# Turned tiles split on VectorE, score groups every eight products, and a first block whose first four places carry no scores

## The chip, the cores and the metric

The kernel runs on one core of one Trainium2 chip. The metric is the device time of one execution in microseconds (us). Before the change it is 1717.77 us, the median of three runs (1717.59 to 1717.90).

## What is computed

```python
def reference(A_x, A_wqkv, A_wo, B_x, B_w_gate, B_w_up, B_w_down):
    xn = _layernorm(A_x)                       # 2048 tokens of 512
    qkv = (xn @ wqkv)                          # 32 heads of 16
    p = softmax(q @ k.T * 16 ** -0.5)          # per head, 2048 x 2048
    s = (p @ v) @ wo
    g = silu(((xn @ w_gate) * (xn @ w_up)) @ w_down)   # 1792 wide
    return A_x + s * g
```

## The kernel before, in words

Every fp32 factor is split into a high and a low part, so that a product is the sum of three: high by high, high by low, low by high. Tokens are 16 tiles of 128, in four chunks (c = 0 to 3) of four tiles. Heads are taken in groups of four; a round is one head group and one chunk of queries.

**The early part** (`early`, L705) makes the layer norm, the keys and queries of the first head pair and all values. It is one stream of 253 steps n: the products of keys and queries of chunk 0, values of tiles 0 to 2, keys of chunk 1 (n = 60 to 71), queries of chunk 1 (72 to 83), values of tile 3, keys of chunk 2 (96 to 107), values of tiles 4 and 5, keys of chunk 3 (132 to 143), and values of tiles 6 to 14. One product is one matmul of 128 x 512. A table `at` says ahead of which n other work is put into the engines' queues: statistics (`ln_stats`, VectorE), normalisation (`ln_apply`, on VectorE for odd tiles under 8, else on ScalarE), and the turn of a tile (`ln_turn`): four transpositions on TensorE into one PSUM bank of tag "x", of which there are two, then on ScalarE a copy `raw` (L249) and the high part `xh` (L250), and on GpSimd the low part `xl` as raw less high (line L63, through which all of GpSimd's and SyncE's calls go). Chunk 0 goes another way: ScalarE writes the high part and VectorE subtracts it from the PSUM bank itself (`ln_low`, L258).

The list `EARLY` (L40) names the steps ahead of which a group of four **own scores** is computed: four matmuls of 48 rows (L609) into four PSUM banks of tag "s", each followed by a maximum on VectorE (`mx`, L611). These scores serve only to find the row maxima. Groups 0 to 3 read the keys of chunk 0, groups 4 to 7 those of chunk 1, groups 8 to 11 those of chunk 2, groups 12 to 15 those of chunk 3. After 64 scores `maxima(0)` reduces them on VectorE and sends the result through DRAM (MD) into the rows of the queries (`qs`).

Keys of a chunk go a long way before a score can read them: ScalarE takes the high part `hl` (L306) and a copy `qr` (L309) out of PSUM, GpSimd subtracts, SyncE stores both parts in DRAM (KD) and, when these have landed, loads them back in another layout (`ks`).

**The main part** runs through 2048 places q (`position`, L904). A place computes the scores of one key tile for one head again, turned (L631), and their exponentials on ScalarE (L633), and beside it one own score of a place that lies LEAD = 86 further on. Turned scores and values share three PSUM banks of tag "st"; own scores now have three. A filler puts the products of projections and of the feed-forward part (L285 and L289, two halves of 64 rows) between the places. Every eight places or so a block multiplies the exponentials with the values (L644). Four places stand ahead of the first block without filler.

All five engines take their instructions in the order in which the program writes them.

Of the kernel before, what the change touches and what calls it, by code (L numbers as in the profile page):

```python
# [22 lines left out]
NC = S // 512  # L23
# [8 lines left out]
LEAD = 86  # L32
CYCLES = 240
AHEAD = range(1, 5)
# [2 lines left out]
EBUFS = 11  # L37
HBUFS = 2
QBUFS = 2
EARLY = [66, 75, 84, 93] + [104 + 37 * n // 4 for n in range(17)]  # L40
EARLY_BUFS = {"s": 4, "x": 2, "f": 2}
BUFS = {"st": 3, "s": 3, "misc": 2}
LOWER, UPPER = slice(0, 64), slice(64, P)
# [5 lines left out]
def body(ctx, tc, x, wqkv, wo, wg, wu, wd, out):  # L49
# [23 lines left out]
    def dma(dst, src):  # L73
        sync.dma_start(dst, src)
# [41 lines left out]
    def psum(tag, name):  # L116
        ps, bufs = fst["ps"]
        return ps.tile([P, 512], F32, tag=tag, name=name, bufs=bufs[tag])
# [45 lines left out]
    def wtile(name):  # L164
        return keep.tile([P, ND, P], F32 if name[-1] == "r" else F32R, name=name, bufs=1 if name[-1] == "r" else 2)
# [19 lines left out]
    def tokens(tt):  # L185

        return raw_x[:, tt] if tt < 8 else V[:, tt, 0:D]

    def load_x(tt):
        dma(tokens(tt), x[tt * P:(tt + 1) * P])  # L190
# [38 lines left out]
    def ln_apply(tt):  # L229
        (mv, r0, e, mr), t = norm[tt]  # L230
        xt = tokens(tt)
        if tt < 8 and tt % 2:
            return nc.vector.tensor_scalar(xt, xt, e[:, t:t + 1], mr[:, t:t + 1], op0=OP.mult, op1=OP.add)
        return nc.scalar.activation(xt, xt, AF.Identity, bias=mr[:, t:t + 1], scale=e[:, t:t + 1])

# [4 lines left out]
    def ln_turn(tt):  # L240
        c, t = divmod(tt, 4)
        xt = tokens(tt)
        norm["x", tt] = pt = psum("x" if c else "s", f"xT{tt}")
        for d in range(ND):
            nc.tensor.transpose(pt[:, d * P:(d + 1) * P], xt[:, d * P:(d + 1) * P], ident)
        hi, lo = [x[c][:, :, t * P:(t + 1) * P] for x in (xh, xl)]
        if c:
            raw = norm["raws"][t]
            nc.scalar.activation(raw, pt, AF.Copy)  # L249
            nc.scalar.activation(hi, pt.rearrange("p (d q) -> p d q", d=ND), AF.Copy)  # L250
            pool.tensor_tensor(lo, raw.rearrange("p (d q) -> p d q", d=ND), hi, op=OP.subtract)
        else:
            nc.scalar.activation(hi, pt.rearrange("p (d q) -> p d q", d=ND), AF.Copy)
# [452 lines left out]
    def early():  # L706

        nc.scalar.activation(look, ones[0:1, 0:1], AF.Sqrt)
        for tt in range(4):
            load_x(tt)  # L710
        wraw = []
        for which in (1, 0):
            wraw.append(wtile(f"w{which}r"))
            dma(wraw[-1], wqkv[:, which * D:which * D + P].rearrange("(d p) f -> p d f", p=P))
        norm["raws"] = raws = [etile() if d < 3 else part_tile() for d in range(ND)]
        for d in range(ND):
            dma(raws[d], wqkv[d * P:(d + 1) * P, 2 * D:])
        for tt in range(4, NT):
            load_x(tt)

        def ahead(m):
            fst["qk", m] = qk_weights(m, 1), qk_weights(m, 0)

        def exp_table(_):
            nc.scalar.activation(look, ones[0:1, 0:1], AF.Exp)

        def warm(n):
            for _ in range(n):
                nc.tensor.matmul(psum("x", "warm"), ident, idle, start=True, stop=True)

        warm(4)
        first = (0, 1), (2, 3)
        for tts in first:
            ln_open(tts)
        ln_stats(0)
        ln_stats(1)
        ln_root(first[0])
        ln_scale(first[0])
        ln_apply(0)
        ln_apply(1)  # L740
        ln_stats(2)
        ln_stats(3)
        ln_turn(0)
        ln_turn(1)
        warm(3)
        ln_root(first[1])
        ln_scale(first[1])
        ln_apply(2)
        last = ln_apply(3)
        ln_low(0)  # L750
        ln_low(1)
        ln_turn(3)
        ln_turn(2)
        ln_low(3)
        ln_low(2)
        wk, wq = [split_raw(f"w{which}", raw, last) for which, raw in zip((1, 0), wraw)]
        wv = [[etile().bitcast(F32R) for _ in range(ND)] for _ in range(2)]
        for d in range(ND):
            nc.scalar.activation(wv[0][d], raws[d], AF.Copy)
            pool.tensor_tensor(wv[1][d], raws[d], wv[0][d], op=OP.subtract)  # L760

        def k(c):
            yield from qk_proj(wk, 0, 1, c, "f")
            load_k(0, [c])

        def q(c):
            yield from qk_proj(wq, 0, 0, c, "f" if c else "x")
            load_q(c)

        def v(*tts):  # L770
            for tt in tts:
                yield from v_proj(wv, tt, "f")

        at = {n: [] for n in range(253)}
        for c, stats, apply, turns in ((1, (0, 2, 4, 6), (26, 26, 26, 26), (38, 42, 46, 50)),
                                       (2, (16, 20, 26, 27), (60, 60, 62, 62), (70, 74, 79, 83)),
                                       (3, (30, 34, 36, 38), (73, 73, 85, 85), (100, 106, 112, 118))):
            for t in range(4):
                for n, fn in ((stats[t], ln_stats), (apply[t], ln_apply), (turns[t], ln_turn)):
                    at[n].append((fn, 4 * c + t))  # L780
        for tts, n, root, scale in ((tuple(range(4, 8)), 0, 13, 25), (tuple(range(8, NT)), 16, 52, 53)):
            at[n].insert(0, (ln_open, tts))
            at[root].append((ln_root, tts))
            at[scale].insert(0, (ln_scale, tts))
        at[190].append((ones_rows, ks[0]))
        at[150].append((exp_table, None))
        at[205].append((ahead, 1))
        at[130] += [(ones_columns, slice(8, NT)), (other_keys, None)]
        fst["v"] = v_proj(wv, NT - 1, "st")
        gens = [k(0), q(0), v(0, 1, 2), k(1), q(1), v(3), k(2), v(4, 5), k(3), v(*range(6, NT - 1))]  # L790
        scored = 0
        stream = (n for g in gens for n in g)
        for n in range(253):
            for fn, arg in at[n]:
                fn(arg)
            if n in EARLY:
                for _ in range(4 if n != EARLY[-1] else LEAD - scored):
                    score(scored, 0)
                    scored += 1
                if scored == 64:  # L800
                    maxima(0)
            next(stream, None)
        assert scored == LEAD
        return wq

    ffp = ExitStack()
# [105 lines left out]
    def position(q):  # L912

        n, j = divmod(q, 4)
        i, kt = divmod(n, NT)
        g, c = divmod(i, NC)
        now[0] = n
        Tied.on = n < 18
        if j == 0:
            if kt == 8 and i + 2 < NU:  # L920
                load_q(i + 2)
            if kt == 0 and g + 1 < NG and c == 1:
                load_k(g + 1)
            ready[n] = i, kt, []
        if j == 3 and kt % 4 == 2:
            step_small(later)
        ready[n][2].append(expo(i, kt, j))
        scored = q + LEAD
        if scored < TOTAL:
            score(scored, 1)  # L930
        step()
        if j == 1:
            prepare()
        if scored < TOTAL and scored % (4 * NT) == 4 * NT - 1:
            reduced.append(lambda: maxima(scored // (4 * NT)))

    TOTAL = NU * NT * 4

    with tc.manual_schedule(engines=ORDERED):
# [2 lines left out]
        ctx.enter_context(banks_of(BUFS))  # L942
        run(fst["v"])
        q = 0
        while q < 4:
            position(q)
            q += 1
        for b in range(NU * NT // 2):
            if fil.done:
                parts = iter([3, 2, 3, 2, 2, 2, 1, 2])  # L950
                fil = Filler(ending(), lambda n: next(parts))
            work = fil.begin()
            if b >= NU * NT // 2 - 2:
                last = TOTAL - 4 * (NU * NT // 2 - 1 - b)
            else:
                fits = min(9, max(7, int(2.6 + 0.62 * work))) if q + LEAD < TOTAL and work else 8
                need = 8 * (b + 1)
                last = min(max(q + fits, need + AHEAD[0]), need + AHEAD[-1], TOTAL - 4)
            count = last - q
            fil.spread(max(2, count - 2))  # L960
            for k in range(count):
                position(q)
                q += 1
                if 0 < k < count - 1 or count < 3:
                    fil.part()
            if b < NU * NT // 2 - 1:
                values([ready.pop(2 * b), ready.pop(2 * b + 1)])
# [33 lines left out]
```

## Time and profile before

| | before |
|---|---|
| median of three runs | 1717.77 us |
| the profiled execution | 1718.17 us |
| its span, first to last instruction | 1716.4 us |
| granted TensorE clock | 0.999 |
| early part, first matmul to first turned score | 2.4 to 101.0 us |
| first block of value products starts | 108.2 us |

In a row of the timeline stand the start in us, the duration in us, the engine, the line, the operation, output and inputs, and how many instructions were merged into the row. Brackets give idle time of that engine ahead of it and what ended it. PE is TensorE, DVE VectorE, ACT ScalarE, POOL GpSimd, SPq the queue of SyncE that issues transfers. A row's duration of several matmuls counts the last one to its end; the next row can start before.

### The profile page before, as it was taken

To read this page: it belongs to the slowest core of one execution; us is meant where nothing else is said; L and a number is where in the kernel's file an instruction comes from. 1 tells how busy PE (TensorE), PEld (TensorE's weight loads), DVE (VectorE), ACT (ScalarE), POOL (GpSimd) and SP (SyncE) were. 2 spreads that over 40 slices of the span, in tenths; PEclk is the share of its full clock that TensorE was granted. 3 is DMA by queue.
4 is the path that set the end of the run, shared out by engine and by line. 5 is a ranking of instruction groups with operands and counts; after the bars stand their busy time and mean duration, and the time that the engine had idled before them with its cause. 6 is when DMAs were issued, how large, how long until landed. Compare 5 with 4: busy or idle time off the path is not lost. (4 is left out here: it accounts for less than half of the span.)

```text
span 1716.4 us, 35005 instructions
## 1 busy us (share of the span) xinstructions
PE 1705.0 (99%) x13574; PEld 1042.5 (61%) x13574; DVE 1435.9 (84%) x2478; ACT 1307.4 (76%) x2568; POOL 885.4 (52%) x889
## 2 busy tenths in 40 slices
PE   8999999999999999999999999999999999999998
PEld 6666656666666665666656565666665666666655
DVE  6778888888888888888888888888888888898933
ACT  6358877877777778778777777887778787777774
POOL 5315445762644638446354572663637546446572
PEclk9999999999999999999999999999999999999999
DMA  6316633620241312412115220320225112011352
GB/s 210 106 48 201 243 115 125 152 66 19 64 91 36 107 47 73 89 47 60 30 52 133 64 74 23 92 71 27 64 75 125 54 36 73 27 54 48 121 177 79
DMA packets 117378, 145.79 MB, mean 85 GB/s; under 512 B 12636, under 2 KB 74332, under 8 KB 114524
## 3 DMA queue, kind: packets, MB, share of 16 engines
q1 hardware_dynamic: 117212, 143.55, 28.5%
q8 instruction: 107, 1.75, 0.4%
q14 instruction: 59, 0.48, 0.1%
HBM read 95.94 MB, written 47.45 MB: 84 GB/s over the span
## 5 line engine op out<-in xcount | busy, mean ns | idle before, releaser
L611 DVE TENSOR_REDUCE mx<-s 128x1 f32<-128x512 f32 x2048 | 1256.1, 683 | 212.3 <-PE s L609 177.4
L633 ACT ACTIVATE e<-t 128x512 f32<-128x512 f32 x2048 | 1100.1, 601 | 99.2 <-PE pv L644 47.4
L631 PE MATMUL t<-qs,ks 50*128 50x512 f32 x2048 | 783.4, 408 | 0.1
L609 PE MATMUL s<-ks,qs 48*128 48x512 f32 x2048 | 771.0, 410 | 0.6 <-DVE mx L611 0.5
L63 POOL TENSOR_TENSOR acc<-acc,part 128x512 f32<-128x512 f32 x214 | 276.3, 1291 | 610.2 <-ACT part L655 609.8
L631 PEld LDWEIGHTS t<-qs,ks 50*128 50x128 f32 x2048 | 359.1, 185 | 276.0 <-issue 118.6
L644 PE MATMUL pv<-e,V 128*32 128x512 f32 x4096 | 492.5, 598 | 0.0
L609 PEld LDWEIGHTS s<-ks,qs 48*128 48x128 f32 x2048 | 350.6, 185 | 28.8 <-issue 5.4
L655 ACT ACTIVATE part<-pv 128x512 f32<-128x512 f32 x214 | 128.1, 599 | 209.7 <-PE pv L644 209.7
L644 PEld LDWEIGHTS pv<-e,V 128*32 128x32 f32 x4096 | 107.0, 109 | 242.0 <-issue 215.9
L289 PE MATMUL g<-fh,w1h 64*128 64x512 f32 x224 | 90.5, 404 | 0.0
L285 PE MATMUL u<-fh,w0h 64*128 64x512 f32 x224 | 90.4, 404 | 0.0
L289 PE MATMUL y<-dh,hh 64*128 64x512 f32 x224 | 89.6, 400 | 0.0
L285 PE MATMUL y<-dh,hh 64*128 64x512 f32 x224 | 88.9, 397 | 0.0
L289 PE MATMUL u<-fh,w0l 64*128 64x512 f32 x224 | 88.2, 394 | 0.0
L289 PE MATMUL g<-fl,w1h 64*128 64x512 f32 x224 | 88.0, 393 | 0.0
L285 PE MATMUL g<-fl,w1h 64*128 64x512 f32 x224 | 88.0, 393 | 0.0
L285 PE MATMUL u<-fh,w0l 64*128 64x512 f32 x224 | 88.0, 393 | 0.0
L285 PE MATMUL u<-fl,w0h 64*128 64x512 f32 x224 | 88.0, 393 | 0.0
L289 PE MATMUL g<-fh,w1l 64*128 64x512 f32 x224 | 87.9, 393 | 0.0
L285 PE MATMUL g<-fh,w1h 64*128 64x512 f32 x224 | 87.9, 392 | 0.0
L289 PE MATMUL u<-fl,w0h 64*128 64x512 f32 x224 | 87.8, 392 | 0.0
(262 smaller groups left out, 2987.5 us busy)
## 6 DMA issues: line engine op xcount, KB each, us to landing
w1r<-in_wg_dram SPq DMA_DIRECT2D x56, 256.0 KB
w0r<-in_wu_dram SPq DMA_DIRECT2D x56, 256.0 KB
wdr<-in_wd_dram SPq DMA_DIRECT2D x56, 256.0 KB
qs<-QD SPq DMA_DIRECT2D x64, 192.0 KB
ks<-KD SPq DMA_DIRECT2D x12, 768.0 KB
KD<-hl SPq DMA_DIRECT2D x16, 512.0 KB
QD<-hl SPq DMA_DIRECT2D x16, 512.0 KB
OD<-acc SPq DMA_DIRECT2D x31, 256.0 KB
```

Of the source, the lines that this page charges most:

```text
L63: got = getattr(self.engine, name)(*args, **kw)
L285: nc.tensor.matmul(outs[k], l[LOWER], r[LOWER], start=k == 0 and n == 0, stop=(stop or k == 0) and n == len(low) - 1, skip_group_check=k == 1)
L289: nc.tensor.matmul(outs[1 - k], l[UPPER], r[UPPER], start=k == 0 and m == 0, stop=(stop or k == 0) and m == len(high) - 1, skip_group_chec ...
L609: nc.tensor.matmul(o, QS[i][b:b + KB, pr, t * P:(t + 1) * P], k[b:b + KB, pr, kc * 512:(kc + 1) * 512], start=True, stop=True)
L611: nc.vector.tensor_reduce(MX[i][:, j, t, kc:kc + 1], o, axis=AX.X, op=OP.max)
L631: nc.tensor.matmul(o, k[b:b + KR, pr, kt * P:(kt + 1) * P], QS[i][b:b + KR, pr], start=True, stop=True)
L633: nc.scalar.activation(e, o, AF.Exp, scale=DH ** -0.5)
L644: nc.tensor.matmul(o[32 * j:32 * j + 32], V[:, kt, h0:h0 + 32], es[j], start=n == 0, stop=n == len(todo) - 1)
L655: nc.scalar.activation(part, o, AF.Copy)
```

## The change

```diff
-EARLY = [66, 75, 84, 93] + [104 + 37 * n // 4 for n in range(17)]
+EARLY = [66, 75, 84, 93] + [102 + 8 * n for n in range(19)]
...
     def ln_apply(tt):
-        if tt < 8 and tt % 2:
+        if tt < 12 and tt % 2:
             return nc.vector.tensor_scalar(xt, xt, e[:, t:t + 1], mr[:, t:t + 1], op0=OP.mult, op1=OP.add)
...
     def ln_turn(tt):
-        if c:
+        if c == NC - 1:
             raw = norm["raws"][t]
...
-                for n, fn in ((stats[t], ln_stats), (apply[t], ln_apply), (turns[t], ln_turn)):
-                    at[n].append((fn, 4 * c + t))
+                for n, fn in ((stats[t], ln_stats), (apply[t], ln_apply), (turns[t], ln_turn), (turns[t] + 3, ln_low)):
+                    if fn is not ln_low or c < NC - 1:
+                        at[n].append((fn, 4 * c + t))
...
-                for _ in range(4 if n != EARLY[-1] else LEAD - scored):
+                for _ in range(4 if n != EARLY[-1] else LEAD + 4 - scored):
...
-        if scored < TOTAL:
+        if 4 <= q and scored < TOTAL:
             score(scored, 1)
...
-        while q < 4:
-            position(q)
-            q += 1
...
-                last = min(max(q + fits, need + AHEAD[0]), need + AHEAD[-1], TOTAL - 4)
+                last = min(max(q + fits, need + AHEAD[0]), need + AHEAD[-1], TOTAL - 4) if b else need + AHEAD[-1]
```

Chunks 1 and 2 now go the way of chunk 0: ScalarE's eight `raw` copies and GpSimd's eight subtractions fall away, and VectorE subtracts out of the PSUM bank three steps after the turn. Tiles 9 and 11 are normalised on VectorE. Groups of own scores stand every eight steps from n = 102, 23 of them in place of 21, and hold 90 scores in place of 86; so the first four places of the main part need none. These four places are part of the first block, among its filler.

On VectorE, at the end of the statistics (rows L203 and L204; `xT` is the PSUM bank of a turned tile, `xl` the low part of chunk 1), the difference of the two orders is:

```order
 L203 BN_STATS st<-V 128x6
 L204 BN_AGGR mv_336<-st 128x2
+L258 TENSOR_TENSOR xl_155<-xT_404,xh_151 128x4x128
+L258 TENSOR_TENSOR xl_155<-xT_418,xh_151 128x4x128
+L258 TENSOR_TENSOR xl_155<-xT_429,xh_151 128x4x128
 L213 RECIPROCAL r_337<-r_337 128x8
```

The three subtractions (the fourth follows the reciprocal) stand behind all sixteen statistics.

On TensorE, at the second and third turn of chunk 1, ahead of steps 42 and 46, with the engine that the row waits for, before:

```order
L245 MATMUL xT_419<-ident,ks_133 128x128 x3
L266 MATMUL v_401<-e,fh 128x512 x2
L266 MATMUL v_401<-e,fl 128x512 x2
L245 MATMUL xT_431<-ident,ks_133 128x128 [waits PE_49,Activation_49]
L245 MATMUL xT_431<-ident,ks_133 128x128 x3
```

and now:

```order
L245 MATMUL xT_418<-ident,ks_133 128x128 x3
L266 MATMUL v_401<-e,fh 128x512 x2
L266 MATMUL v_401<-e,fl 128x512 x2
L245 MATMUL xT_429<-ident,ks_133 128x128 [waits DVE_49]
L245 MATMUL xT_429<-ident,ks_133 128x128 x3
```

The third turn, which takes the bank of the first one, waited for ScalarE (and TensorE's own end) and now waits for VectorE.

On TensorE, around group 12, the first that reads the keys of chunk 3, before (`v_857` are the values of tile 8, 24 products behind the last of these keys):

```order
L266 MATMUL v_857<-e,xh_152 128x512 x8
L266 MATMUL v_857<-e,xl_156 128x512 x2
L609 MATMUL s_12_0_868<-ks_132,qs 128x512
L609 MATMUL s_12_1_871<-ks_132,qs 128x512
L609 MATMUL s_12_2_874<-ks_132,qs 128x512
L609 MATMUL s_12_3_877<-ks_132,qs 128x512
```

and now (`v_823` are the values of tile 7, 12 products behind them):

```order
L266 MATMUL v_823<-e,xh_151 128x512 x6
L266 MATMUL v_823<-e,xl_155 128x512 x2
L609 MATMUL s_12_0_846<-ks_132,qs 128x512
L609 MATMUL s_12_1_849<-ks_132,qs 128x512
L609 MATMUL s_12_2_852<-ks_132,qs 128x512
L609 MATMUL s_12_3_855<-ks_132,qs 128x512
```

Group 12 stands 34 products behind the last product of these keys before, and 22 now (two of tile 7's stand ahead of group 11); between them lie three other groups before and two now.

On TensorE, at the start of the main part (`t` is a turned score, `s` an own score, `p` a filler's product), before:

```order
L631 MATMUL t_0_0_1109<-qs,ks_132 128x512
L609 MATMUL s_5_3_1113<-ks_132,qs 128x512
L631 MATMUL t_0_1_1116<-qs,ks_132 128x512
L609 MATMUL s_5_2_1120<-ks_132,qs 128x512
L631 MATMUL t_0_2_1123<-qs,ks_132 128x512
L609 MATMUL s_6_1_1127<-ks_132,qs 128x512
L631 MATMUL t_0_3_1130<-qs,ks_132 128x512
L609 MATMUL s_6_0_1134<-ks_132,qs 128x512
```

and now:

```order
L631 MATMUL t_0_0_1113<-qs,ks_132 128x512
L631 MATMUL t_0_1_1117<-qs,ks_132 128x512
L285 MATMUL p_0_2_1121<-xh_152,w0h 128x512
L289 MATMUL p_0_3_1122<-xh_153,w0h 128x512
L285 MATMUL p_0_2_1121<-xl_156,w0h 128x512
L289 MATMUL p_0_3_1122<-xl_157,w0h 128x512
L631 MATMUL t_0_2_1127<-qs,ks_132 128x512
L285 MATMUL p_0_2_1121<-xh_152,w0l 128x512
```

From the first turned score to the first block there are 12 turned scores and 24 filler products in both; own scores are 12 before and 8 now. From the first block to the end TensorE's instructions stand in the same order in both kernels.

More of the change, by code (lines that the diff above doesn't have):

```diff
@@ L802, in early @@
             next(stream, None)
-        assert scored == LEAD
+        assert scored == LEAD + 4
         return wq
```

## The prediction

> **What bounds the kernel now.** I read the page first, then TensorE's busy time in a later stretch of 20 us, then the timeline of the first 110 us engine by engine.
>
> ```profile
> PE 1705.0 (99%) x13574; PEld 1042.5 (61%) x13574; DVE 1435.9 (84%) x2478; ACT 1307.4 (76%) x2568; POOL 885.4 (52%) x889
> ...
> 160.00:180.00 20.00, 20.00 (x170) 12.65 (x168) 17.92 (x31) 16.40 (x33) 7.61 (x9) 1.00 1.06 285
> ```
>
> TensorE (PE, the number behind the width) has no idle time even there, where the DMA share is 1.06. From the first block of values on its instructions stand in the same order in both kernels. So what the change is worth is by how much that first block, at 108.17 us, moves, and everything behind shifts with it. I go through the early part place by place.
>
> **First place, the turns of chunk 1 (cost 2.75).** VectorE's statistics are behind TensorE:
>
> ```profile
> 26.58 0.18 DVE L204 BATCH_NORM_AGGREGATE mv<-st 128x2 f32<-128x6 f32 x1
> ...
> 10.91 1.28 DVE L258 TENSOR_TENSOR fl<-xT,fh 128x512 fp32r<-128x512 f32 x2
> ...
> 24.63 0.60 PE L245 MATMUL xT<-ident,ks 128*128 128x128 f32 x4
> ```
>
> The last statistics were queued at step 38 and end with this aggregate at 26.7. The new subtraction of the first turned tile stands behind them and takes 1.28 / 2 = 0.64, to 27.3. The third turn, which ran at 24.63, needs that bank and now waits until about 27.4: 2.75 later. Behind it in TensorE's queue stands everything else, and ScalarE's high parts wait for it. The fourth turn then finds its bank free (second subtraction at 28.0, turn at 28.8). Nothing earlier in VectorE's queue goes, so I see no lower price than 2.6 here if the order holds.
>
> **What goes in exchange, up to step 84 (gain 1.1).**
>
> ```profile
> 30.27 0.94 PE L609 MATMUL s<-ks,qs 48*128 48x512 f32 x4
> 31.14 0.74 PE L266 MATMUL p<-xh,w1l 128*128 128x512 f32 x2
> ...
> 33.34 0.72 PE L266 MATMUL p<-xh,w0h 128*128 128x512 f32 x2
> ...
> 34.66 0.73 PE L609 MATMUL s<-ks,qs 48*128 48x512 f32 x4
> ...
> 37.03 0.86 PE L266 MATMUL p<-xl,w0h 128*128 128x512 f32 x3
> 39.06 0.66 PE L245 MATMUL xT<-ident,V 128*128 128x128 f32 x4 [1.17 <-ACT xh L250]
> ...
> 32.71 0.58 ACT L350 ACTIVATE V<-v 128x512 f32<-128x512 f32 x1
> ...
> 35.19 2.49 DVE L611 TENSOR_REDUCE mx<-s 128x1 f32<-128x512 f32 x4 [1.91 <-PE s L609]
> ```
>
> Group 0 took 30.27 to 31.14, 0.87, where later groups take 0.66: its queries were still landing. 2.75 later they are there: -0.2. The queries' products at 33.34 start 0.46 after the product ahead of them rather than 0.23, for a PSUM bank that ScalarE empties until 33.3 and that will be empty by then: -0.2. The turn at 39.06 would have started at 37.7 and waited for ScalarE; ScalarE now has no raw copies and half the normalisations there, but the bank of this turn is freed by a subtraction on VectorE that stands behind the maxima of group 1. That group starts at 34.66 + 2.3 = 37.0 (34.66 is its row), its maxima begin 0.53 later (35.19) and take 2.49, to 40.0, the subtraction at 40.6. TensorE is there at 37.7 + 2.3 = 40.0 and waits 0.6 instead of 1.3: -0.7. GpSimd's eight subtractions of 1.3 hid behind this and free nothing that is waited for. So step 84 moves by 2.75 - 0.2 - 0.2 - 0.7 = **+1.65**.
>
> From the other side: were VectorE's queue empty at 24.6, the 2.75 would be 0, the queries would still be landing at 30.3, and -0.9 would be left.
>
> **The groups (gain 0.25, and 1.1 in new waits).**
>
> ```profile
> 65.92 0.74 PE L609 MATMUL s<-ks,qs 48*128 48x512 f32 x4
> ...
> 68.83 0.73 PE L609 MATMUL s<-ks,qs 48*128 48x512 f32 x4
> ...
> 71.95 0.73 PE L609 MATMUL s<-ks,qs 48*128 48x512 f32 x4
> ...
> 66.45 2.48 DVE L611 TENSOR_REDUCE mx<-s 128x1 f32<-128x512 f32 x4 [0.41 <-PE s L609]
> ...
> 95.77 0.73 PE L609 MATMUL s<-ks,qs 48*128 48x512 f32 x4
> 97.04 1.10 PE L609 MATMUL s<-ks,qs 48*128 48x512 f32 x2 [0.55 <-DVE mx L611]
> 98.07 2.11 PE L266 MATMUL v<-e,xh 128*128 128x512 f32 x8
> ...
> 83.80 0.22 DVE L615 TENSOR_REDUCE m<-mx 128x16 f32<-128x64 f32 x1
> ...
> 84.52 2.44 DVE L611 TENSOR_REDUCE mx<-s 128x1 f32<-128x512 f32 x4
> ```
>
> Nine products and a group take 2.91 (65.92 to 68.83), ten 3.12 (to 71.95): a product 0.23, a group 0.83, and eight products with one 2.67. Two more groups of four cost 1.65. The last group had six scores and took 95.77 to 98.07, some 2.4 with its switch and the wait for VectorE; two scores take about 0.5. Sum -0.25.
>
> VectorE's four maxima take 2.48 and had 0.41 idle in a period of 2.91; in 2.67 there is 0.19. They end 3.0 after their group's start, so 0.34 after the next group's start, when its fourth score, 0.34 in, wants that bank: between 0 and 0.25 lost per group, 0 to 4 in all. The nearest row is the end of the six-score group, where the fifth score waits for a first maximum; the fourth score waits less, and a period that has waited leaves the next without a wait. I take 0.4. After group 15 `maxima(0)` puts 0.72 between the maxima (83.80 to 84.52); with 0.19 to spare it reaches the fourth score two groups later, 0.7 (0 to 1.0). Together **+1.1**. It also moves ahead of the weight loads for the next head pair in SyncE's queue; these are first used behind the first block, 20 us away.
>
> **The keys (cost 4.0).** Groups 8 and 12 read keys that have just been made, and they now stand 7 and 12 steps earlier.
>
> ```profile
> 60.73 0.97 PE L266 MATMUL p<-xl,w1h 128*128 128x512 f32 x3
> ...
> 61.78 0.60 ACT L306 ACTIVATE hl<-p 128x512 fp32r<-128x512 f32 x1 [3.11 <-PE p L266]
> ...
> 63.00 1.30 POOL L63 TENSOR_TENSOR hl<-qr,hl 128x512 fp32r<-128x512 f32 x1 [6.79 <-issue]
> ...
> 64.33 0.82 SPq L63 DMA_DIRECT2D KD<-hl  x2
> 67.64 0.79 SPq L63 DMA_DIRECT2D ks<-KD  x2
> ...
> 41.62 0.79 SPq L63 DMA_DIRECT2D ks<-KD  x2
> ...
> 42.52:44.52 2.00, 2.00 (x10) 1.17 (x9) 1.54 (x3) 0.83 (x3) 1.60 (x2) 1.00 0.79 197
> ...
> 26.79 0.79 SPq L63 DMA_DIRECT2D qs<-QD  x2
> ...
> 46.70 0.73 PE L609 MATMUL s<-ks,qs 48*128 48x512 f32 x4
> ...
> 47.93 0.60 PE L245 MATMUL xT<-ident,V 128*128 128x128 f32 x4
> 48.29 0.72 PE L266 MATMUL p<-xl,w1h 128*128 128x512 f32 x2
> ...
> 60.06 0.73 PE L609 MATMUL s<-ks,qs 48*128 48x512 f32 x4
> ...
> 55.66 0.80 SPq L63 DMA_DIRECT2D ks<-KD  x2
> ```
>
> The last product of chunk 3's keys starts at 60.73 + 0.97 - 0.40 = 61.3, their load is issued at 67.64, 6.34 later. None of that chain changes. From issue to use no row tells directly: the same load at 41.62 moved its bytes until 44.5, so at least 2.9; group 12 at 71.95 did not wait, so at most 4.3; the queries issued at 26.79 released the second score of group 0 near 30.5, which is 3.7, the same kind of load, and I take that. So keys are there 10.0 after their last product. Group 12 now comes three periods of 2.67 after group 9, which stands two products ahead of the end of these keys: 8.0 less 1.0 until that last product starts, 7.0. Wait 3.0 (2.2 to 3.6).
>
> For chunk 2, from the turn at 47.93 to the load at 55.66 are 7.7, with the landing 11.4. Group 8 now comes four periods of 2.67 and three turns of 0.36 (47.93 to 48.29) after group 4, this turn a group and four products, 1.7, after group 4: 10.1. By the same sum groups 4 and 8 stand 4 x 0.83 + 37 x 0.23 + 3 x 0.36 = 12.9 apart before, and the rows show 13.4 (46.70 to 60.06); so I take 10.4. Wait 1.0 (0.2 to 1.6). Behind each wait stands all of TensorE's queue, and VectorE idles. Together **+4.0** (2.4 to 5.2).
>
> [...]
>
> **The first block (gain 1.35).**
>
> ```profile
> 101.02 0.50 PE L631 MATMUL t<-qs,ks 50*128 50x512 f32 x1
> ...
> 101.59 7.38 DVE L611 TENSOR_REDUCE mx<-s 128x1 f32<-128x512 f32 x12 [1.62 <-PE t L631]
> ...
> 101.68 4.28 ACT L633 ACTIVATE e<-t 128x512 f32<-128x512 f32 x8
> ...
> 108.17 1.92 PE L644 MATMUL pv<-e,V 128*32 128x512 f32 x16
> ```
>
> From the first turned score to the block are 7.15. VectorE's twelve maxima run without a gap, 0.61 each, and own scores wait for their three banks: VectorE is the limit. Now there are eight own scores, the first four places away. TensorE then has 24 steps of 0.23 (12 turned scores, own ones beside them, 12 filler pairs), 5.5, plus 0.3 to change to the block; exponentials at 4.28 / 8 = 0.53 allow the twelfth turned score 5.2 after the first. What is late next is both, at about 5.8: **-1.35** (-0.7, if exponentials pace it at 0.6, to -1.6).
>
> **Sum.** 1.65 - 0.25 + 1.1 + 4.0 - 1.35 = +5.15. Against its own execution of 1718.17 (span 1716.4 and 1.8 around it) that is 1723.3; that execution was 0.4 over the median, so I forecast a median of 1717.77 + 5.15 = 1722.9.
>
> **Rivals.**
> 1. The keys land at the early bound (2.9): +3.55, 1721.3. For: the bytes had moved by then. Against: the queries' row.
> 2. VectorE is not behind: the subtraction runs when the high part is ready, near 23.5. Then the first place costs 0 and 1.65 becomes -0.9: +2.6, 1720.4. Against: six statistics back to back until 26.7, and the order.
> 3. Not slower: the delay is absorbed later, in the stretch around 160 to 180 us where stores of `xh` fill the DMA engines (share 1.06). If TensorE waits there for a transfer, up to all 5.15 vanish and the time is 1717.8; it decides once that wait is as long as the delay. Against: 20.00 busy of 20.00.
> 4. VectorE becomes the limit of the groups: every period waits 0.25 for the fourth bank, 20 times, +4.5 more: 1727.5. For: 0.19 to spare. Against: waits of the keys let VectorE catch up twice.
>
> **Chances.** Forecast 0.74, rival 1 0.09, rival 2 0.07, rival 3 0.05, rival 4 0.05. The range takes the landing's bounds (1721.3 to 1724.1), rival 2 with both bounds low, and most of rival 4: 1719.5 to 1726.5. A measurement of this kernel can tell about 0.2%, 3.4 us, from no change; so slower begins at 1721.2. Slower: forecast, rival 4 and half of rival 1, 0.83; within: 0.16; faster: 0.01, since even without the first place and both key waits the sum is -1.4.
>
> **What would show it.** Right: an idle stretch of TensorE of about 2.7 at the third turn of chunk 1, released by VectorE's L258; group 8 and group 12 released by a DMA, about 1 and 3; the first block 5.8 after the first turned score and about 5 later than 108.17; the rest shifted as a whole. Wrong: no wait at group 12 (then the landing is short), or the third turn at 24.6.

## The result and the profile after

| | before | after |
|---|---|---|
| median, runs side by side | 1717.90 us (5 runs, 1717.59 to 1718.40) | 1725.57 us (5 runs, 1722.64 to 1728.07) |
| profiled execution | 1718.17 us | 1725.57 us |
| its span | 1716.4 us | 1723.5 us |
| its mean granted clock | 0.999 | 0.997 |
| first turned score | 101.02 us | 110.67 us |
| first block of value products | 108.17 us | 116.60 us |

The ratio of the runs is 1.0041 (95% interval 1.0031 to 1.0052). The kernel became slower by 7.7 where 5.15 was forecast; 1725.57 lies inside the range, 2.7 over the predicted 1722.9. The second thing to see is the scatter: 0.8 before, 5.4 after.

The page of the changed kernel, three of its lines (PE's busy time, the granted clock in 40 slices of 43 us, and own scores):

```profile
PE 1708.2 (99%) x13574; PEld 1044.9 (61%) x13574; DVE 1440.4 (84%) x2488; ACT 1301.8 (76%) x2558; POOL 874.9 (51%) x881
...
PEclk9999999999999999999999999999999999999999
...
L609 PE MATMUL s<-ks,qs 48*128 48x512 f32 x2048 | 772.5, 412 | 2.8 <-DMA ks<-KD 2.6
```

The line of own scores on the page of before:

```profile
L609 PE MATMUL s<-ks,qs 48*128 48x512 f32 x2048 | 771.0, 410 | 0.6 <-DVE mx L611 0.5
```

Own scores now wait 2.6 for keys on their way through DRAM, where before their idle time was 0.6, most of it for VectorE. PE is busy 3.2 longer (1705.0 before) with the same 13574 instructions, so some of them ran longer. The clock row shows nothing: a slice averages 43 us.

The timeline of TensorE in the changed kernel, at the places that the prediction named:

```profile
27.77 0.66 PE L245 MATMUL xT<-ident,ks 128*128 128x128 f32 x4 [2.58 <-DVE xl L258]
...
41.04 0.63 PE L245 MATMUL xT<-ident,V 128*128 128x128 f32 x4 [0.52 <-DVE xl L258]
...
61.41 0.70 PE L609 MATMUL s<-ks,qs 48*128 48x512 f32 x3 [0.35 <-DMA ks<-KD]
...
74.59 2.02 PE L609 MATMUL s<-ks,qs 48*128 48x512 f32 x4 [2.23 <-DMA ks<-KD]
76.54 1.22 PE L266 MATMUL v<-e,xl 128*128 128x512 f32 x2
77.56 2.76 PE L266 MATMUL v<-e,xh 128*128 128x512 f32 x6
80.25 1.22 PE L609 MATMUL s<-ks,qs 48*128 48x512 f32 x4
81.40 0.77 PE L266 MATMUL v<-e,xh 128*128 128x512 f32 x2
...
110.67 0.51 PE L631 MATMUL t<-qs,ks 50*128 50x512 f32 x2
...
116.60 1.92 PE L644 MATMUL pv<-e,V 128*32 128x512 f32 x16
```

The third turn waits 2.58 for VectorE, the later one 0.52 where it waited 1.17 for ScalarE, and the scores of groups 8 and 12 wait for keys. Then comes something that the prediction has nowhere: two products take 1.22 and six take 2.76, where two take 0.77 a little later. Behind group 12 the granted clock is 0.50 until 81.50 (below).

The timeline of VectorE shows what the third turn waits for, and the first block's own maxima:

```profile
26.95 0.18 DVE L204 BATCH_NORM_AGGREGATE mv<-st 128x2 f32<-128x6 f32 x1
27.05 1.26 DVE L258 TENSOR_TENSOR xl<-xT,xh 128x512 fp32r<-128x512 f32 x2
...
113.03 4.88 DVE L611 TENSOR_REDUCE mx<-s 128x1 f32<-128x512 f32 x8 [5.28 <-PE s L609]
```

The two first subtractions stand directly behind the last aggregate of the statistics, and the turn starts when the first of them is done. The eight maxima of the first block start 2.4 behind the first turned score (110.67); VectorE idles 5.28 ahead of them.

The columns of the next view are a stretch, its length, busy time and instructions of PE, PEld, DVE, ACT and POOL, the granted clock, the DMA share and GB/s. The stretches are cut where the records of the granted clock change (74.68, 81.50) and in steps of 3.413 from there:

```profile
23.48:26.89 3.41, 1.70 (x10) 1.08 (x8) 3.27 (x9) 0.94 (x2) 0.00 (x0) 1.00 0.65 238
...
71.26:74.68 3.42, 1.19 (x6) 0.68 (x5) 1.38 (x3) 0.00 (x0) 0.00 (x0) 1.00 0.54 119
74.68:78.09 3.41, 3.27 (x8) 1.85 (x9) 2.56 (x4) 0.29 (x1) 0.00 (x0) 0.50 0.10 15
78.09:81.50 3.41, 3.41 (x11) 1.82 (x9) 0.44 (x2) 0.30 (x1) 0.00 (x0) 0.50 0.00 0
81.50:84.92 3.42, 3.42 (x15) 2.35 (x16) 2.97 (x6) 0.60 (x1) 0.00 (x0) 1.00 0.00 0
```

In the stretch in which TensorE waits for group 12's keys it is busy 1.19 of 3.42. The granted clock is 0.50 for the two stretches behind it, then 1.00 again. The wait of the third turn left 1.70 busy in its stretch, and no half clock followed. Where a later execution has no change of the clock in its early part, its stretches are counted back in steps of 3.413 from the one at the kernel's end, where TensorE has finished: the clock falls to 0.50 there, at 1719.90 in this execution and at 1712.30 in that of before. The two ways agree: in this execution the change at the end is 1645.22 behind 74.68, or 482 steps.

### The profile page after: what moved, and what is told of

It is laid out like the page before. It is cut to its first block, busy times and chain, and to the rows that moved or that the text cites. A ratio compares the mean times of both kernels' runs of the same rounds, so it can differ in the third digit from the quotient of the medians.

```text
span 1723.5 us, 34987 instructions
## 1 busy us (share of the span) xinstructions
PE 1708.2 (99%) x13574; PEld 1044.9 (61%) x13574; DVE 1440.4 (84%) x2488; ACT 1301.8 (76%) x2558; POOL 874.9 (51%) x881
## 5 line engine op out<-in xcount | busy, mean ns | idle before, releaser
L289 PE MATMUL g<-fh,w1h 64*128 64x512 f32 x224 | 90.7, 405 | 0.0
L285 PE MATMUL y<-dh,hl 64*128 64x512 f32 x224 | 87.9, 393 | 0.0
L285 PE MATMUL u<-fl,w0h 64*128 64x512 f32 x224 | 87.9, 392 | 0.0
L285 PE MATMUL y<-dl,hh 64*128 64x512 f32 x224 | 87.9, 392 | 0.0
```

What stands on the lines that cost most here:

```text
L285: nc.tensor.matmul(outs[k], l[LOWER], r[LOWER], start=k == 0 and n == 0, stop=(stop or k == 0) and n == len(low) - 1, skip_group_check=k == 1)
L289: nc.tensor.matmul(outs[1 - k], l[UPPER], r[UPPER], start=k == 0 and m == 0, stop=(stop or k == 0) and m == len(high) - 1, skip_group_chec ...
```

## Experiments

The theory from here on: the prediction's terms hold, and the 2.7 beyond them is a half clock that follows a long wait in some runs. The rivals: a term is mis-sized by that much, or the clock falls for a reason that has nothing to do with the waits.

**The changed kernel again.** No edit, a second set of runs.

> The changed kernel once more, with the four terms of the theory in view: a wait of some 2.6 us at the third turn of chunk 1, waits for keys at groups 8 and 12 of some 0.4 and 2.2 us, a first block 5.9 us after the first turned score, and, behind the wait at group 12, some 7 us at half the granted clock. If the half clock hangs on how the wait falls against a window of the clock's own, the time scatters over some 5 us from run to run, between 1722.5 (mean clock 0.999) and 1728 (0.997); if it belongs to the kernel, all runs agree within 1 us.

Measured 1726.29 (1723.78 to 1726.89, 5 runs), ratio 1.0043 (1.0030 to 1.0055). The profiled execution has a half clock of 6.82 behind group 12, at 75.08. The runs spread over 3.1, those of the kernel before beside them over 1.9 (22 runs). So neither the half clock nor the wide scatter was an accident of the first set.

**Groups 4 to 12 at their steps of before.**

```diff
-EARLY = [66, 75, 84, 93] + [102 + 8 * n for n in range(19)]
+EARLY = [66, 75, 84, 93, 104, 113, 122, 132, 141, 150, 159, 169] + [178 + 8 * n for n in range(10)] + [252]
```

> The changed kernel with groups 4 to 12 back at the steps of before (group 8 at 141, group 12 at 178) and eight steps apart behind that. Theory (waits for keys, and a half clock behind the longer one): both waits go, the clock stays whole (0.999) and with it the scatter; the third turn still waits 2.6. 1.65 - 0.25 + 0.9 - 1.35 = +0.95 against before: 1718.9, between 1718 and 1720, all runs within 1 us. Rival one (VectorE's added subtractions and maxima are the cost): no change, 1724 to 1726. Rival two (the half clock comes of the wait at the third turn): 1721.5 with a mean clock of 0.997.

Measured 1719.84 (1718.79 to 1723.44, 11 runs), ratio 1.0011 (1.0002 to 1.0020). No score waits for a key. The third turn keeps its wait, and no half clock follows in the profiled execution. But the runs did not agree within 1 us, as expected: six with a mean clock of 0.999 or 1.000 are at 1718.79 to 1719.84, and five with 0.998 at 1720.96 to 1723.44. The wait of the third turn is the one that is left to bring this. Its timeline of TensorE:

```profile
27.42 0.66 PE L245 MATMUL xT<-ident,ks 128*128 128x128 f32 x4 [2.60 <-DVE xl L258]
```

The stretches of 3.413, cut as above:

```profile
22.75:26.16 3.41, 2.07 (x11) 1.36 (x10) 3.27 (x10) 1.33 (x3) 0.00 (x0) 1.00 0.85 298
26.16:29.58 3.42, 2.16 (x14) 1.89 (x15) 2.46 (x5) 1.19 (x3) 0.20 (x1) 1.00 0.45 117
```

Here the boundary of two stretches falls in the middle of the wait, and each keeps over 2 of busy time. Moving the groups is what costs the most: without it 6.45 of the 7.87 above the kernel before are gone (1726.29, 1719.84 and 1718.42 side by side).

**Chunk 1 turned in the old way.**

```diff
-        if c == NC - 1:
+        if c in (1, NC - 1):
...
-                    if fn is not ln_low or c < NC - 1:
+                    if fn is not ln_low or c == 2:
```

> The changed kernel with chunk 1 turned as before (raw copy on ScalarE, subtraction on GpSimd); chunk 2 and the rest as changed. Theory: the third turn of chunk 1 does not wait, step 84 stands 0.9 earlier than before in place of 1.6 later, and the rest, waits for keys and half clock included, is as in the changed kernel: 2.5 less than that, about 1723 with the same scatter. Rival (what is saved early is waited for at groups 8 and 12, since keys land at their own time): within 0.5 us of the changed kernel, the wait at group 12 longer by 2.

Measured 1723.62 (1722.77 to 1725.93, 6 runs), ratio 1.0032 (1.0020 to 1.0044). The wait at the third turn is gone, those for keys stay. The timeline of TensorE in this kernel:

```profile
58.14 0.47 PE L609 MATMUL s<-ks,qs 48*128 48x512 f32 x1 [0.34 <-DMA ks<-KD]
...
72.15 0.47 PE L609 MATMUL s<-ks,qs 48*128 48x512 f32 x1 [2.13 <-DMA ks<-KD]
```

The stretches of 3.413, cut as above:

```profile
70.27:73.68 3.41, 1.07 (x4) 0.48 (x4) 0.80 (x2) 0.00 (x0) 0.00 (x0) 1.00 0.52 118
73.68:77.09 3.41, 3.41 (x9) 2.48 (x8) 1.78 (x3) 0.61 (x1) 0.00 (x0) 0.50 0.05 6
```

The wait at group 12 suffices by itself for a half clock; here it lasts one stretch. The rival, that what is saved early is waited for at the keys, holds for little of it: counted from the first turn of chunk 1, group 2 starts at 17.35 and group 12 at 50.38, in the changed kernel with a whole clock (below) at 19.65 and 52.42, so 2.04 of the 2.30 are still there at group 12.

**Both undone**: the late groups and the old chunk 1 together, so that the first block, chunk 2 and two more groups are left of the change.

> Both edits at once: chunk 1 turned as before and groups 4 to 12 at the steps of before; left of the change are chunk 2 on VectorE, two normalisations, the two groups more and the first block. Theory (terms add up): -0.9 - 0.25 + 0.9 - 1.35 = -1.6 against before: 1716.3, with a whole clock and runs within 1 us. Rival (the gain of the first block is waited for later): 1717.9, as before.

Measured 1718.56 (1718.16 to 1719.42, 11 runs), ratio 1.0001 (0.9993 to 1.0010), mean clock 0.999 in every run. With both waits gone, scatter and half clock are gone too. The gain that the sum promised did not come: from group 2 to the first turned score it lost 1.44 against the kernel before (62.58 against 61.14), where 0.65 was worked out. The next two kernels ask which part lost it.

**The first block alone**, with its 23 groups, on the turns of before.

```diff
-EARLY = [66, 75, 84, 93] + [104 + 37 * n // 4 for n in range(17)]
+EARLY = [66, 75, 84, 93, 104, 113, 122, 132, 141, 150, 159, 169] + [178 + 8 * n for n in range(10)] + [252]
...
```

Behind the dots stand the lines of the first block, as in the change.

> The kernel before with the first block of the change and its 23 groups, of which groups 0 to 12 stay at their steps of before and ten follow every eight products; turns and normalisation as before. Theory: the first block gives 1.2, two more groups net of the shorter last one and the waits of VectorE cost 0.65 to 1.4, so the time is 0.6 less to 0.2 more than before, ratio 0.9996 to 1.0001. Rival, that the 1.4 lost between group 2 and the first turned score in the kernel with both undone came from VectorE's new subtractions: here it is 0.4 or less, and the time 0.8 to 1.0 less.

Measured 1718.96 against 1718.60 beside it (10 runs), ratio 1.0001 (0.9992 to 1.0010), no change that the runs can tell. Its timeline of TensorE, group 12, the last group and the first turned score:

```profile
73.16 0.73 PE L609 MATMUL s<-ks,qs 48*128 48x512 f32 x4
...
99.80 0.94 PE L609 MATMUL s<-ks,qs 48*128 48x512 f32 x2
103.63 0.50 PE L631 MATMUL t<-qs,ks 50*128 50x512 f32 x2
```

Group 2 starts at 41.05, so the way to the first turned score is 62.58 again: the groups lost the 1.44, not the subtractions on VectorE. From group 12 to the last group are 26.64 (before: 71.95 to 95.77, 23.82), so two more groups and the small waits of VectorE cost 2.82, for which 1.65 + 1.1 stood in the prediction. From the last group to the first turned score are 3.83 (before 5.25): its four scores fewer give 1.42, where 1.9 was taken. That is 0.5 of the miss; the rest of it is that I had priced the small waits of these few groups at less than those of the whole change.

**VectorE's part alone**: chunks 1 and 2 subtracted on VectorE, tiles 9 and 11 normalised there, groups and first block of before.

```diff
-        if tt < 8 and tt % 2:
+        if tt < 12 and tt % 2:
...
-        if c:
+        if c == NC - 1:
...
+                for n, fn in ((stats[t], ln_stats), (apply[t], ln_apply), (turns[t], ln_turn), (turns[t] + 3, ln_low)):
+                    if fn is not ln_low or c < NC - 1:
+                        at[n].append((fn, 4 * c + t))
```

> The kernel before with the turned tiles' part of the change alone: chunks 1 and 2 subtracted on VectorE, tiles 9 and 11 normalised there; groups and first block as before. Theory: the third turn of chunk 1 waits 2.6 behind the statistics, the later turn waits 0.5 in place of 1.17 and group 0 no longer waits for its queries, +1.6 at group 2 and the same at the first block, about 1720.0 where before has 1718.4, ratio 1.0009; if the wait of 2.6 also lets the clock fall in some runs, those stand 1.5 to 3 higher still. Rival, that the wait is given back further on because VectorE's queue empties: first block less than 0.5 later, ratio 1.0003 or less.

Measured 1720.72 (1719.12 to 1723.35, 10 runs) against 1718.60, ratio 1.0012 (1.0003 to 1.0021). The five runs with a mean clock of 0.999 or 1.000 are at 1719.12 to 1719.90, the five with 0.998 at 1721.54 to 1723.35. The profiled one is of the latter; its timeline of TensorE:

```profile
28.50 1.11 PE L245 MATMUL xT<-ident,ks 128*128 128x128 f32 x4 [2.58 <-DVE xl L258]
29.27 1.20 PE L266 MATMUL v<-e,fl 128*128 128x512 f32 x2
```

The stretches of 3.413, cut as above:

```profile
24.94:28.35 3.41, 0.98 (x5) 0.44 (x3) 3.27 (x9) 0.60 (x1) 0.20 (x1) 1.00 0.53 202
28.35:31.77 3.42, 3.27 (x12) 2.78 (x13) 1.38 (x3) 1.20 (x2) 0.00 (x0) 0.50 0.52 120
```

The same wait of 2.6 as in the kernel with the late groups now lies within one stretch, which has 0.98 of busy time left, and the next stretch runs at half clock. From the first turn of chunk 1 to group 2 it takes 21.16 here (22.95 to 44.11) and 19.62 there (21.86 to 41.48): **one half-clock stretch cost 1.54**.

**The parts without a wait**: chunk 2's turns and the first block as in the change, with LEAD 82, so that the 21 groups stay where they were.

```diff
-LEAD = 86
+LEAD = 82
...
-                for _ in range(4 if n != EARLY[-1] else LEAD - scored):
+                for _ in range(4 if n != EARLY[-1] else LEAD + 4 - scored):
...
-        if scored < TOTAL:
+        if 4 <= q and scored < TOTAL:
...
```

Behind the dots stand chunk 2's turns, the two normalisations and the rest of the first block, as in the change.

> The kernel before with three parts of the change that bring no wait: chunk 2 turned in the new way (chunk 1 in the old), the first block with its four places and without their own scores, and LEAD 82 in place of 86, so that the early part keeps its groups and steps of before (21 groups, the last with six scores, 86 in all). Theory, that both the key waits and the two more groups were costs of moving groups, and that chunk 2's turns (0.7) and the first block (1.2) are gains by themselves: 1.9 less than the kernel before beside it, ratio 0.9989, first block about 106.3 after allowing for the start. Rival, that splitting chunk 2 on VectorE, and not the more numerous groups, cost the 0.8 that the kernel with both undone lost between group 2 and the first turned score: 1.1 less, ratio 0.9994.

Measured 1717.48 (1716.49 to 1718.48, 11 runs) against 1718.60, ratio 0.9992 (0.9984 to 1.0001). From the first turn of chunk 1 (23.29) to the first block (107.72) are 84.43, before 86.34: 1.9 less, as the theory had it. The median moved by 1.1 only, which its interval doesn't tell from no change, and 1.1 is what the rival gave. The trace speaks against the rival: from group 2 (40.66) to the first turned score (101.79) are 61.13, before 61.14, so the subtractions cost nothing there. In this execution the row of the opening in TensorE's timeline hides the gain; before:

```profile
2.40 5.29 PE L729 MATMUL warm<-acc,ident 128*128 128x512 f32 x8 [2.40 <-POOL acc L63]
```

and this kernel:

```profile
2.40 6.74 PE L729 MATMUL warm<-acc,ident 128*128 128x512 f32 x8 [2.40 <-POOL acc L63]
```

The same eight opening records take 1.45 longer in this execution, and everything behind starts that much later. Whether this also holds the median down is not shown, since the openings of the other runs are not on record.

**Group 12's wait filled**: two matmuls, which nothing reads, in the idle stretch.

```diff
+            if n == 166:
+                warm(2)
```

A matmul of this kind stands as two records in a row of the timeline (the four of the opening as eight).

> The changed kernel with two matmuls more, ahead of group 12, whose result nothing reads (two matmuls of the same kind take 0.86 each in the opening of the changed kernel's timeline, 1.72 together). They stand in the stretch of 2.23 in which TensorE idles for the keys, so about 0.5 of idle time is left and the first score of group 12 starts when it did. Theory, that the half clock of 3.41 or 6.83 behind group 12 comes from this idle stretch: the clock stays whole there, the first block stands 2.5 to 3 earlier than in the changed kernel when it has the half clock, the median is 1722 to 1723.5, and the runs lie closer together than 1722.6 to 1728. First rival, that the clock falls for a reason that has nothing to do with idle time (its own rhythm, or the load of all engines): half clock in most runs, 1725.6 and the same scatter. Second rival, that the loads of the keys, not the clock, are what varies: the clock whole, but the time still 1725.

Measured 1725.42 (1723.47 to 1726.34, 5 runs), ratio 1.0038 (1.0026 to 1.0051): no better than the changed kernel. The timeline of TensorE around group 12:

```profile
75.09 1.88 PE L729 MATMUL warm<-acc,ident 128*128 128x512 f32 x4
77.49 0.47 PE L609 MATMUL s<-ks,qs 48*128 48x512 f32 x1 [0.52 <-DMA ks<-KD]
```

The stretches of 3.413, cut as above:

```profile
25.52:28.93 3.41, 0.82 (x4) 0.35 (x3) 3.27 (x10) 0.36 (x1) 0.20 (x1) 1.00 0.43 163
28.93:32.35 3.42, 3.42 (x13) 2.93 (x13) 1.07 (x2) 1.20 (x2) 0.00 (x0) 0.50 0.41 117
...
76.72:80.13 3.41, 2.47 (x10) 1.43 (x10) 1.94 (x4) 0.35 (x1) 0.00 (x0) 1.00 0.23 30
```

Behind the filled wait the clock stays whole. But now the other wait, of the third turn, lies within one stretch with 0.82 busy, and the half clock comes there. The expected median was wrong because it left out this second place: four of the five runs have a mean clock of 0.998. In the one run with a mean clock of 1.000 the time is 1723.47.

**Both waits filled.** The next three ran side by side; the kernel before took 1718.84 (12 runs).

```diff
...
+            if n == 46:
+                warm(2, "s")
...
+            if n == 166:
+                warm(2)
```

> The changed kernel with two matmuls more ahead of the third turn of chunk 1 and two more ahead of group 12, whose results nothing reads; both waits keep their length and hold about 0.9 of idle time each. Theory: the granted clock is set for one window of 3.413 at a time by what TensorE did in the window before (all half-clock stretches so far are one or two such windows, and start a whole number of windows after the clock first rose); a window with 2.2 or more of idle time gives a half window next, one with 1.9 or less does not, and where the windows lie differs from run to run. With both waits filled no window holds 1.9, so the clock stays whole in every run until the tail; the median is 1722.5 to 1724, all runs within 2 of one another, each half window that is gone being worth 1.7. Rival, that the clock falls for another reason than idle time: half-clock stretches as before, median 1725.5, scatter 3 to 5.

Measured 1723.82 (1722.75 to 1724.51, 7 runs), ratio 1.0030 (1.0018 to 1.0041), mean clock 0.999 or 1.000 in every run. The timeline of TensorE at the two waits:

```profile
28.23 0.66 PE L245 MATMUL xT<-ident,ks 128*128 128x128 f32 x4 [0.88 <-DVE xl L258]
...
75.34 0.46 PE L609 MATMUL s<-ks,qs 48*128 48x512 f32 x1 [0.48 <-DMA ks<-KD]
```

The stretches of 3.413, cut as above:

```profile
24.37:27.79 3.42, 2.98 (x11) 1.49 (x9) 3.28 (x10) 0.60 (x1) 0.10 (x1) 1.00 0.63 225
...
72.16:75.58 3.42, 2.94 (x10) 1.41 (x8) 1.19 (x2) 0.00 (x0) 0.00 (x0) 1.00 0.52 119
```

With two pairs of useless matmuls the scatter is 1.8 where the kernel without them, side by side (below), has 4.4. The median is 1.3 lower, but the intervals of the two ratios overlap, so a gain in time is not shown. The delay that is left is 4.98.

**One matmul in each wait in place of two.**

```diff
...
+            if n == 46:
+                warm(1, "s")
...
+            if n == 166:
+                warm(1)
```

> The same with one matmul more at each place in place of two: about 1.7 of idle time is left at the third turn and 1.4 at group 12. Theory, that a window must hold more than 1.9 of idle time: still no half window ahead of the tail in any run, median 1722.5 to 1724, as with both places filled. Rival, that any pause of some 1.3 can let the clock fall where it meets a window badly: half windows in some runs, median 1724 to 1726 and scatter over 3.

Measured 1723.85 (1722.74 to 1726.30, 6 runs), ratio 1.0033 (1.0022 to 1.0045). Four runs are as with both filled (1722.74 to 1723.92), two have a mean clock of 0.998 and take 1725.77 and 1726.30. The profiled one is of the four. Its stretches around the third turn and around group 12:

```profile
23.79:27.21 3.42, 2.42 (x11) 1.38 (x9) 3.25 (x10) 0.81 (x2) 0.00 (x0) 1.00 0.64 230
27.21:30.62 3.41, 2.68 (x16) 2.32 (x17) 1.96 (x4) 1.70 (x4) 0.20 (x1) 1.00 0.51 120
71.58:74.99 3.41, 2.05 (x8) 1.02 (x6) 1.45 (x3) 0.00 (x0) 0.00 (x0) 1.00 0.54 120
74.99:78.41 3.42, 3.01 (x12) 1.90 (x12) 2.58 (x4) 0.60 (x1) 0.00 (x0) 1.00 0.11 15
```

TensorE is idle for 1.73 in the first two together and for 1.77 in the last two. Wherever the boundary falls there, a stretch of 3.413 keeps about 1.64 of busy time or more, and has no more than 1.8 of idle time. So, if the waits were as long in the two slower runs, 1.9 of idle time in a stretch is not the bound that I took it for: some stretch with less let the clock fall. No trace of these two runs is kept, so which one is not known.

**The changed kernel beside them.**

> The changed kernel once more, beside the two filled ones on one chip. Theory: a half-clock stretch of 3.41 or 6.83 after the third turn or after group 12 in most runs, 1724 to 1728, median 1725.6. Rival, that this chip keeps its clock whole whatever the kernel does: 1722.5 to 1724, the same as both filled kernels, which then say nothing.

Measured 1725.09 (1723.04 to 1727.45, 5 runs), ratio 1.0037 (1.0024 to 1.0049). Its profiled execution, 1723.04, happens to keep the clock whole. The stretch that ends in group 12's wait, and the next:

```profile
70.49:73.90 3.41, 1.64 (x8) 1.02 (x6) 1.92 (x4) 0.00 (x0) 0.00 (x0) 1.00 0.50 131
73.90:77.31 3.41, 2.73 (x11) 1.84 (x12) 2.44 (x4) 0.60 (x1) 0.00 (x0) 1.00 0.12 19
```

The timeline of TensorE in the same execution, the rows that answer to the terms of the prediction:

```profile
27.39 0.66 PE L245 MATMUL xT<-ident,ks 128*128 128x128 f32 x4 [2.60 <-DVE xl L258]
...
41.48 0.73 PE L609 MATMUL s<-ks,qs 48*128 48x512 f32 x4
...
57.27 0.88 PE L609 MATMUL s<-ks,qs 48*128 48x512 f32 x4
...
60.27 0.47 PE L609 MATMUL s<-ks,qs 48*128 48x512 f32 x1
...
63.85 0.73 PE L609 MATMUL s<-ks,qs 48*128 48x512 f32 x4
...
69.39 0.73 PE L609 MATMUL s<-ks,qs 48*128 48x512 f32 x4
...
74.25 0.47 PE L609 MATMUL s<-ks,qs 48*128 48x512 f32 x1 [2.11 <-DMA ks<-KD]
75.05 0.71 PE L609 MATMUL s<-ks,qs 48*128 48x512 f32 x3 [0.34 <-DMA ks<-KD]
...
77.73 0.73 PE L609 MATMUL s<-ks,qs 48*128 48x512 f32 x4
...
107.78 0.51 PE L631 MATMUL t<-qs,ks 50*128 50x512 f32 x2
```

The wait is as long as in the execution that lost its clock (2.11 and 2.23), but the boundary at 73.90 cuts it, and 1.64 of busy time is left ahead of the boundary. This execution is the right one to hold against the terms of the prediction, since the first turn of chunk 1 stands at 21.83 in it and in the profile of before.

## Why the prediction was near, and what it lacked

Each term against the execution with a whole clock (1723.04, before 1718.17):

| term | predicted | measured | from |
|---|---|---|---|
| step 84 (group 2) | +1.65 | +1.60 | 39.88 to 41.48 |
| group 8's keys | +1.0 | +1.2 | 57.27 to 60.27 to 63.85: 3.00 and 3.58, less 2.67 each |
| group 12's keys | +3.0 | +3.0 | 69.39 to 74.25 to 77.73: 4.86 and 3.48, less 2.67 each |
| other groups, small waits | +0.85 | +0.9 | 61.14 to 66.30 from group 2 to the first turned score, less the keys |
| first block | -1.35 | -1.2 | 7.15 to 5.92 |
| sum at the first block | +5.15 | +5.5 | 108.17 to 113.70 |

- **The turns.** The third turn came 2.76 later (24.63 to 27.39; predicted 2.75), behind the last aggregate, as the order said. The later turn, at 40.69, waits 0.52 in place of 1.17 (predicted 0.6 and 1.3).
- **The keys.** The landing taken from the queries' row, 3.7 after the issue, was near enough: in the profiled execution of the result the load for group 12 is issued at 71.43, the first score starts 3.2 behind it (74.59) and the other three 4.0 (75.42). In the execution of the table the wait at group 12 comes in two parts, 2.11 ahead of the first score and 0.34 ahead of the other three; for the rest of the 3.0, some 0.55, no row names a releaser. At group 8 a row names the DMA for 0.41 of the 1.2; for the rest no row names a releaser, so a part of it may not be the keys'.
- **The groups.** The sum is right by two errors: the shorter last group gives 1.4 and not 1.9, and in the changed kernel the small waits of VectorE cost less than where no key wait lets it catch up (0.9 against 1.44 for the groups as a whole). VectorE did not become the limit.
- **The first block.** 5.92, not 5.8. Of the two limits named for it ScalarE is the nearer one: in the profiled execution of the result, where the first block starts 5.93 after the first turned score, eleven exponentials run in one stretch of 5.49, 0.50 each.
- **Little absorption.** Most of the delay stayed: from the first block to the end of the span are 1607.6 here and 1608.2 before (1606.9 in the profiled execution of the result). So 0.7 to 1.3 came back later; what gave it back is not known.

What the prediction lacked is in its sum: it took each wait at its own length ("Behind each wait stands all of TensorE's queue, and VectorE idles") and let TensorE go on at full clock behind it. In 11 of the changed kernel's 15 runs on three occasions the mean clock is 0.997 or 0.998, and they take 1723.82 to 1728.07, median 1726.3. In the other four it is 0.999, and they take 1722.64, 1723.04, 1723.18 and 1723.78: the forecast of 1722.9. The missing term is one or two half-clock stretches of 3.41 us, of which one cost 1.54 in the kernel with VectorE's part alone and two cost 2.5 in the profiled execution of the result (88.46 from chunk 1's first turn to the first turned score, against 85.95 with the clock whole). That 1725.57 still fell into the range was in part luck: the upper end of 1726.5 was made from rival 4, which did not come true, nothing in it stood for the clock, and two of the five runs (1726.66 and 1728.07) lie above it.

That the waits bring it is shown by the runs: by the mean clock and the times none of the 7 runs with both waits filled had it, nor any of the 11 with both waits removed, and in the profiled executions, ahead of the kernel's end, it always comes directly behind a stretch that one of the waits had left with 0.82 to 1.20 of busy time. Stretches with 1.50 (in the first repeat of the changed kernel) and more were followed by a full clock. Which it is depends on where the boundaries fall, and they fall differently from run to run: with VectorE's part alone one stands 0.15 ahead of the third turn (28.35, 28.50), in the result's execution 0.88 ahead of it (26.89, 27.77). (The mean clock alone decides no single run: it is rounded to 0.001, about what one half-clock stretch takes from it, and it holds the end of the kernel too.)

The end shows the same thing without any of the waits. Behind its last matmul TensorE stays idle, and the clock falls at the end of the stretch in which it has finished: in before that is 1708.88 to 1712.30, with 1.46 of busy time, in the result 1716.48 to 1719.90, with 0.96. Since 1.46 was followed by a half clock and 1.50 was not, the bound lies near 1.5 of busy time in 3.413 in these traces.

The half-clock stretches seen here last 3.41 and 6.82, one or two steps of 3.413, and in the result's execution the later change stands a whole number of these steps behind them (81.50 to 1719.90, 480 steps). What sets the steps is not shown.

Open stay the exact bound (two runs of the kernel with one matmul in each wait had a half clock by their mean, where their kernel's trace leaves at least 1.64 at the two waits), and why the half clock lasts two stretches in two of the profiled executions and one in three, although TensorE was busy for 3.27 and 3.21 in the first of the two. The two that lasted longer have the fewest matmuls in their first half-clock stretch (7 and 8, against 9, 12 and 13); no run tested whether that is the reason.

## What to carry to other kernels

TensorE's waits of 2.1 to 2.6 cost about their length here (with 2.60 the third turn came 2.76 later), and in a part of the runs 1.5 to 2.5 more behind them: when a change that moves work earlier creates such a wait, look at the granted clock in stretches of a few us behind it and at the scatter of the runs, since the slices of the profile's page don't show it. When a group of scores is moved towards the products that feed it, work out first how long its data are under way; here the two waits for keys (4.2) cost over three times what the first block gave (1.2). The parts that brought no wait (chunk 2's turns, the first block) gave their 1.9 in the trace, and 1.1 in the median, which the runs don't tell from no change.

## What the runs showed of the hardware

- In the result's profiled execution the granted clock falls at 74.68, rises at 81.50 and falls at 1719.90: 2 and 480 units of 3.413 us. Where the units begin differs between executions: the first repeat of the same kernel has its fall at 75.08. The same opening, from 2.40 on, took 5.29 in one profiled execution and 6.74 in another, 1.45 apart, which is as large as the terms argued about here; profiles of two kernels are best compared from the first turn of chunk 1 on.
- Two matmuls without use in each of the two waits kept the clock: by the mean clock none of the 7 runs fell, where 11 of the 15 of the changed kernel did. The medians side by side are 1723.82 and 1725.09.
